# A two-layer SiLU block on one core: zero matmuls at the start, finer loads, plain 128-row matmuls, a split last tile

## The chip, the cores and the metric

The kernel runs on one core of a Trainium2 chip. The metric is the device time of one execution in microseconds (us). Most readings below are taken from a profile of one execution. The span of a profile is about 2 us shorter than the device time of the same execution (135.5 against 137.31 us for the kernel before). Different experiments ran on different chips. Each therefore comes with runs of the kernel before from the same chip, and ratios are taken against those.

## The reference

```python
B, S, D, F = 1, 2048, 640, 1728          # bf16
def reference(x, w1, w2):
    h = jnp.einsum("bsd,df->bsf", x, w1)
    h = silu(h)
    return jnp.einsum("bsf,fd->bsd", h, w2)
```

F is 13.5 times 128. The last block of F has only 64 rows, and both kernels have to deal with that.

## The kernel before

It has two stages, and between them h (transposed, bf16) stays on chip. The w1 stage computes 4 chunks of 512 rows of x times 14 blocks of F. Each block takes five 128x512 matmuls, then a sigmoid on ACT and a product on DVE. The w2 stage computes 16 row tiles of 128 rows. Each row tile has two halves of 320 columns and 13.5 blocks of F.

The start: one x transpose by DMA, then w1 in five row pieces, all from the sync queue.

```python
    nc.sync.dma_start_transpose(out=xT[0][:, :, :], in_=xf[0:NCHUNK, :])     # 512 rows
    for dk in range(DT):                                                     # five pieces of w1
        nc.sync.dma_start(out=w1_sb[:, dk, 0:F], in_=w1r[:, dk, :])
    for c in range(1, SC):
        nc.sync.dma_start_transpose(out=xT[c][:, :, :], in_=...)
    # ... then w2
```

The half block: the last 64 columns of w1 are doubled, so rows 0 to 63 and rows 64 to 127 of the last h block hold the same thing. Output half A takes the lower rows and half B the upper rows, and the two 64-row matmuls can run side by side: both start at 100.58 us in the seam shown below.

```python
        for ft in range(13):
            nc.tensor.matmul(psA[:, :], lhsT=hT_sb[:, ft, s0 : s0 + P], rhs=w2_sb[:, ft, 0:EH], ...)
            nc.tensor.matmul(psB[:, :], lhsT=hT_sb[:, ft, s0 : s0 + P], rhs=w2_sb[:, ft, EH:E], ...)
        nc.tensor.matmul(psA[:, :], lhsT=hT_sb[0:64, 13, s0 : s0 + P],   rhs=w2_sb[0:64, 13, 0:EH], ...)
        nc.tensor.matmul(psB[:, :], lhsT=hT_sb[64:128, 13, s0 : s0 + P], rhs=w2_sb[64:128, 13, EH:E], ...)
        nc.scalar.activation(out=o_sb[:, 0:EH], in_=psA[:, :], func=ACT.Copy)
        nc.vector.tensor_copy(out=o_sb[:, EH:E], in_=psB[:, :])
        nc.sync.dma_start(out=of[s0 : s0 + P, :], in_=o_sb[:, :])
```

## Time and profile before

| | us |
|---|---|
| device time, median of 4 runs | 137.6 (137.3 to 138.24) |
| span of the profile | 135.5 |
| first matmul | 7.32 |
| w2 stage begins | 69.79 |
| last eviction begins | 132.05 |

The page of the kernel before, its busy times and the chain that ended last. TensorE (PE) is the bound, and DVE and ACT are hidden behind it.

```profile
PE 124.3 (92%) x723; PEld 68.5 (51%) x728; DVE 46.2 (34%) x73; ACT 41.5 (31%) x74; POOL 0.7 (0%) x5
PE 92%; DMA 3%; SPq 2%; issue 0%; DVE 0%; DVEq 0%
```

A busy PE is not a PE at full speed. The timeline of the weight loads (PEld) of the kernel before, from the first one on, shows this. Columns: start us, length us, engine, line, operation, operands, count, and in brackets the idle time before with its cause.

```profile
7.31 0.13 PEld L104 LDWEIGHTS <-w_sb 128*128 128x128 bf16 x2 [7.31 <-DMA w_sb<-in_w_dram]
7.72 0.15 PEld L104 LDWEIGHTS <-w_sb 128*128 128x128 bf16 x1 [0.28 <-issue]
8.80 0.13 PEld L104 LDWEIGHTS <-w_sb 128*128 128x128 bf16 x2 [0.93 <-DMA w_sb<-in_w_dram]
...
10.49 0.15 PEld L104 LDWEIGHTS <-w_sb 128*128 128x128 bf16 x1 [0.28 <-issue]
10.92 0.15 PEld L104 LDWEIGHTS <-w_sb 128*128 128x128 bf16 x1 [0.28 <-issue]
11.30 10.68 PEld L104 LDWEIGHTS <-w_sb 128*128 128x128 bf16 x50 [0.23 <-issue]
```

The loads at 10.49 and 10.92 us stand 0.43 us apart with no data wait between them (0.15 us of load and 0.28 of "issue"). From 11.3 us on, 50 follow in 10.68 us, which is 0.216 us from one start to the next. So TensorE ran at half its later pace for the 4.0 us from 7.31 to 11.30; below this is called half clock, or cold. The page's granted-clock row shows full clock in these slices, so on the page the cold stretch can be seen only in the spacing and the durations of the instructions (mostly 634 ns for a matmul, 379 later).

At the warm rate the 280 matmuls of the stage take 60.4 us (280 x 0.2157). The first matmul of the w2 stage, from the timeline of PE:

```profile
69.79 0.30 PE L131 MATMUL psA<-w_sb,hT_sb 128*128 128x320 bf16 x1
```

The second thing to read is the seam between two row tiles, from the timeline of the kernel before:

```profile
100.21 0.30 PE L131 MATMUL psA<-w_sb,hT_sb 128*128 128x320 bf16 x1
100.34 0.30 PE L138 MATMUL psB<-w_sb,hT_sb 128*128 128x320 bf16 x1
100.57 0.09 PEld L148 LDWEIGHTS <-hT_sb 64*128 64x128 bf16 x1 [0.26 <-issue]
100.58 0.31 PE L148 MATMUL psA<-w_sb,hT_sb 64*128 64x320 bf16 x1
100.58 0.31 PE L155 MATMUL psB<-w_sb,hT_sb 64*128 64x320 bf16 x1
100.82 0.31 PE L131 MATMUL psA<-w_sb,hT_sb 128*128 128x320 bf16 x1
100.97 0.30 PE L138 MATMUL psB<-w_sb,hT_sb 128*128 128x320 bf16 x1
```

Read the starts, because the lengths overlap. Plain neighbours start 0.13 to 0.14 us apart. The pair does start at one instant, but 0.24 us after its predecessor, and the next matmul comes another 0.24 us later.

The end of the kernel before, from its timeline: eviction, issue of the store, and then nothing until the span ends at 135.5.

```profile
132.01 0.44 ACT L178 ACTIVATE o_sb<-psA 128x320 bf16<-128x320 f32 x1 [3.44 <-PE psB L155]
132.05 0.49 DVE L179 CAST o_sb<-psB 128x320 bf16<-128x320 f32 x1 [3.39 <-PE psB L155]
132.60 0.33 SPq L180 DMA_DIRECT2D out_dram<-o_sb  x1
```

### The profile page before, as it was taken

Reading aid. Unit: us, or ns where it says so; the run is one execution under the profiler, and the core shown is the slowest. Engines: PE = TensorE matmul, PEld = TensorE weight load, DVE = VectorE, ACT = ScalarE, POOL = GpSimd, SP = SyncE. Lnnn points to the kernel's source line nnn. Section 1 sums busy time; section 2 is a strip of 40 time slices with the busy share of each in tenths; the row PEclk is TensorE's granted clock in tenths of the full one; section 3 lists DMA queues with packets and bytes.
Section 4 is the critical chain, followed back from the end, with each engine's and each line's share of the span. In section 5 each row is a group of like instructions: output and inputs, shape, how many; then the busy total and the mean of one; then the engine's idle time right before and its main releaser. Section 6 shows DMA issues by size and latency. Waiting matters only on the chain.

```text
span 135.5 us, 1791 instructions
## 1 busy us (share of the span) xinstructions
PE 124.3 (92%) x723; PEld 68.5 (51%) x728; DVE 46.2 (34%) x73; ACT 41.5 (31%) x74; POOL 0.7 (0%) x5
## 2 busy tenths in 40 slices
PE   0089999999999999999999999999999999999990
PEld 0024444444444444444456666666666666666650
DVE  0000976666666666666661001111110111111101
ACT  4000855555555555555551001111110011111101
POOL 0001000000000000000000000000000000000000
PEclk9999999999999999999999999999999999999997
DMA  3999999900000000000000111110011111101111
GB/s 69 269 371 316 212 197 303 349 10 0 0 0 2 0 0 5 0 2 0 0 0 0 53 48 48 48 48 23 30 48 48 48 48 53 48 13 36 48 48 48
DMA packets 15239, 9.81 MB, mean 72 GB/s; under 512 B 10752, under 2 KB 14592, under 8 KB 15232
## 3 DMA queue, kind: packets, MB, share of 16 engines
q1 hardware_dynamic: 15232, 9.71, 24.5%
q8 instruction: 5, 0.08, 0.3%
q14 instruction: 2, 0.02, 0.0%
HBM read 4.46 MB, written 2.62 MB: 52 GB/s over the span
## 4 chain that ended last, share of the span: by engine, by line
PE 92%; DMA 3%; SPq 2%; issue 0%; DVE 0%; DVEq 0%
PE ps L104 46%; PE psA L131 22%; PE psB L138 21%; PE psA L148 3%; DMA w_sb<-in_w_dram 3%; SPq L65 2%; DVE o_sb L179 0%; PE psB L155 0%; DVEq L179 0%
## 5 line engine op out<-in xcount | busy, mean ns | idle before, releaser
L104 PE MATMUL ps<-xT,w_sb 128*128 128x512 bf16 x275 | 62.3, 387 | 7.6 <-DMA w_sb<-in_w_dram 7.3
L131 PE MATMUL psA<-w_sb,hT_sb 128*128 128x320 bf16 x208 | 57.1, 300 | 0.0
L138 PE MATMUL psB<-w_sb,hT_sb 128*128 128x320 bf16 x208 | 56.9, 299 | 0.0
L117 DVE TENSOR_TENSOR hT_sb<-ps,sig 128x512 bf16<-128x512 f32 x56 | 38.3, 691 | 32.2 <-ACT sig L112 32.2
L104 PEld LDWEIGHTS <-w_sb 128*128 128x128 bf16 x280 | 27.5, 99 | 41.9 <-DMA w_sb<-in_w_dram 8.8
L112 ACT ACTIVATE sig<-ps 128x512 f32<-128x512 f32 x56 | 33.0, 598 | 35.3 <-PE ps L104 35.3
L179 DVE CAST o_sb<-psB 128x320 bf16<-128x320 f32 x16 | 7.9, 492 | 53.4 <-PE psB L155 53.4
L131 PEld LDWEIGHTS <-hT_sb 128*128 128x128 bf16 x208 | 20.3, 98 | 9.6
L138 PEld LDWEIGHTS <-hT_sb 128*128 128x128 bf16 x208 | 20.4, 98 | 7.4
L178 ACT ACTIVATE o_sb<-psA 128x320 bf16<-128x320 f32 x16 | 7.0, 438 | 54.9 <-PE psB L155 54.9
L148 PE MATMUL psA<-w_sb,hT_sb 64*128 64x320 bf16 x16 | 4.9, 307 | 0.0
L155 PE MATMUL psB<-w_sb,hT_sb 64*128 64x320 bf16 x16 | 4.9, 307 | 0.0
L148 PEld LDWEIGHTS <-hT_sb 64*128 64x128 bf16 x16 | 1.5, 93 | 4.2 <-issue 4.2
L63 ACT ACT_TABLE_LOAD x1 | 1.3, 1283 | 0.7 <-PEq L195 0.7
L155 PEld LDWEIGHTS <-hT_sb 64*128 64x128 bf16 x16 | 1.5, 93 | 0.0
L87 POOL COPY w_sb<-w_sb 128x320 bf16<-128x320 bf16 x1 | 0.5, 451 | 11.8 <-DMA w_sb<-in_w_dram 11.8
L61 DVE MEMSET warm<- 128x1 f32 x1 | 0.1, 59 | 0.8 <-PEq L195 0.8
L63 ACT ACTIVATE warm<-warm 128x1 f32<-128x1 f32 x1 | 0.2, 203 | 0.0
L195 POOL MEMSET const-uint8-127<- 128x1 uint8 x1 | 0.1, 103 | 0.0
L195 POOL MEMSET const-bfloat16-1.0<- 128x1 bf16 x1 | 0.1, 102 | 0.0
L195 POOL MEMSET const-float32-0.0<- 128x1 f32 x1 | 0.1, 99 | 0.2 <-issue 0.2
L195 POOL MEMSET const-float32-1.0<- 128x1 f32 x1 | 0.1, 99 | 0.0
## 6 DMA issues: line engine op xcount, KB each, us to landing
out_dram<-o_sb SPq DMA_DIRECT2D x16, 160.0 KB, 1.8
w_sb<-in_w_dram SPq DMA_DIRECT2D x5, 432.0 KB, 5.2
w_sb<-in_w_dram SPq DMA_DIRECT2D x1, 2080.0 KB, 9.0
w_sb<-in_w_dram SPq DMA_DIRECT2D x1, 80.0 KB, 8.5
xT<-in_x_dram SPq DMA_TRANSPOSE x4, 5.7
w_sb<-in_w_dram SPq DMA_DIRECT2D x1, 40.0 KB, 7.9
```

Of the source, the lines that this page charges most:

```text
L63: nc.scalar.activation(out=warm2[:, :], in_=warm[:, :], func=ACT.Sigmoid)
L65: nc.sync.dma_start_transpose(out=xT[0][:, :, :], in_=xf[0:NCHUNK, :])
L87: nc.gpsimd.tensor_copy(out=w1_sb[:, :, F:F_PAD], in_=w1_sb[:, :, F - F_REM : F],)
L104: nc.tensor.matmul(ps[:fw, :], lhsT=w1_sb[:, dk, f0 : f0 + fw], rhs=xT[c][:, dk, :], start=(dk == 0), stop=(dk == DT - 1),)
L112: nc.scalar.activation(out=sig[:fw, :], in_=ps[:fw, :], func=ACT.Sigmoid,)
L117: nc.vector.tensor_tensor(out=hT_sb[:fw, ft, s0 : s0 + NCHUNK], in0=ps[:fw, :], in1=sig[:fw, :], op=ALU.mult,)
L131: nc.tensor.matmul(psA[:, :], lhsT=hT_sb[:, ft, s0 : s0 + P], rhs=w2_sb[:, ft, 0:EH], start=(ft == 0), stop=(ft == last),)
L138: nc.tensor.matmul(psB[:, :], lhsT=hT_sb[:, ft, s0 : s0 + P], rhs=w2_sb[:, ft, EH:E], start=(ft == 0), stop=(ft == last),)
L148: nc.tensor.matmul(psA[:, :], lhsT=hT_sb[0:F_REM, ft, s0 : s0 + P], rhs=w2_sb[0:F_REM, ft, 0:EH], start=(ft == 0), stop=True,)
L155: nc.tensor.matmul(psB[:, :], lhsT=hT_sb[F_REM : 2 * F_REM, ft, s0 : s0 + P], rhs=w2_sb[F_REM : 2 * F_REM, ft, EH:E], start=(ft == 0), sto ...
L178: nc.scalar.activation(out=o_sb[:, 0:EH], in_=psA[:, :], func=ACT.Copy)
L179: nc.vector.tensor_copy(out=o_sb[:, EH:E], in_=psB[:, :])
```

## The change

It has four parts, with one intent: shorten the parts of PE's chain that are not dense full-speed matmuls.

1. Twelve matmuls on a zeroed tile run while the first loads are under way (warm-up).
2. The first 512 rows of x become two chunks of 256. w1 comes in column blocks of 256, 256, 384 and 832 columns, so that the first block suffices for ten matmuls.
3. The half block of F is padded with zeros to 128 rows. Each row tile but the last (see 4) is then 28 plain matmuls.
4. The last row tile is computed as 320, 160 and 160 columns, each with its own eviction and store, so that only 160 columns remain at the very end.

The core of the diff:

```diff
+    NWARM = 12
+    nc.gpsimd.memset(wz[:, :], 0.0)
+    for i in range(NWARM):
+        nc.tensor.matmul(wps[:, :], lhsT=wz[:, 0:P], rhs=wz[:, :], ...)
+    if F_REM:
+        nc.gpsimd.memset(w1_sb[:, :, F:F_PAD], 0.0)
+        nc.gpsimd.memset(w2_sb[F_REM:P, FT_FULL, :], 0.0)
-    nc.sync.dma_start_transpose(out=xT[0][:, :, :], in_=xf[0:NCHUNK, :])
-    for dk in range(DT):
-        nc.sync.dma_start(out=w1_sb[:, dk, 0:F], in_=w1r[:, dk, :])
-    for c in range(1, SC):
-        nc.sync.dma_start_transpose(...)
+    nc.sync.dma_start_transpose(out=xT[0][:, :, :], in_=xf[s0 : s0 + n0, :])   # 256 rows
+    load_w1(0, 2 * P)
+    load_w1(2 * P, 4 * P)
+    load_w1(4 * P, 7 * P)
+    load_x(1)                                                                 # 256 rows
+    load_w1(7 * P, F)
+    for c in range(2, len(chunks)):
+        load_x(c)                                                             # 512 rows each
...
+    order = [(0, ft) for ft in range(7)] + [(1, ft) for ft in range(7)]
+    order += [(0, ft) for ft in range(7, FT)] + [(1, ft) for ft in range(7, FT)]
+    order += [(c, ft) for c in range(2, len(chunks)) for ft in range(FT)]
...
-            # the pair of 64-row matmuls for the last block of F
+            for ft in range(FT):      # 14 plain blocks, psA and psB
...
+        else:                         # last row tile
+            ranges = [(0, EH), (EH, EQ), (EH + EQ, EQ)]
+            for ri, (e0, ew) in enumerate(ranges):
+                ...                   # 14 matmuls, eviction and store of these columns alone
```

## The prediction

> **What bounds the kernel now.** TensorE: the chain of waits is 92% PE, the rest DMA (3%) and the sync queue (2%) before the first matmul. The timeline shows four stretches of the 135.5 us span:
> - 0 to 7.3 us: PE idle until the first w1 piece lands (wait list).
> - 7.3 to 11.3 us: about 8 matmuls. They last 609 to 634 ns against 379 later: PE is cold, besides two DMA waits (0.93 and 0.54 us).
> - 11.3 to 70 us: w1 stage, one 128x512 matmul per 0.216 us, no gaps. All 280 take 60.4 us: as if started warm at 70.0 - 60.4 = 9.6 us.
> - 70 to 131.9 us: w2 stage, 3.88 us per row tile, then evict, store, finish: 3.6 us.
>
> DVE (34%) and ACT (31%) hide.
>
> **What the change does.**
> 1. Start. The first x transpose has 256 rows, not 512, and w1 comes in column blocks (256, 256, 384, 832), the first enough for ten matmuls. The old transpose held the sync queue 2.77 us; half should hold it 1.5. The first w1 block (327 KB) then lands at about 5.5 us (estimate from 3.7 us issue-to-landing of the old first piece).
> 2. Warm-up. Twelve zero matmuls start once GpSimd has filled their tile, about 1.4 us. [...] Nine cold at 0.427 us and three warm end at 6.0 us; all cold, 6.6. So real work starts at about 6.3 us, warm, with the warm-up, not data, as the last gate.
> 3. Two 256-column chunks: 140 matmuls at about 0.109 us replace 70 at 0.216: +0.2 us. ACT and DVE (estimates 0.38 and 0.43 us, scaled from 598/438 and 691/492 ns) keep under PE's 0.55 us per tile.
> 4. DMA now feeds PE just in time. At 280 GB/s (278 in 2 to 9 us) block 3 lands at 8.2 us against a need at 8.5, x chunk 1 at 9.3 against 10.1. I allow 0.4 us of stalls.
> Stage 1 then ends near 67.2 us: **2.7 us saved**.
> 5. The paired 64-row matmuls go. They are not cheap: from the psB before to the psA after, 0.48 us pass, where plain matmuls at 0.1355 would take 0.407. A tile of 28 plain ones takes 3.79 us instead of 3.88: 0.085 x 15 = **1.3 us saved**.
> 6. Last tile: 28 matmuls of 160 columns. Weight loads last 98 ns, so I take 0.08 us each, not 0.069: +0.3 us, repaid by the shorter last eviction and store. Net 0.
>
> All of it lies on PE's chain.
>
> **Predicted: 133.6 us** (137.6 - 2.7 - 1.3), range 132.3 to 135.2. Faster by over 2%: 0.82; within 2%: 0.17; slower: 0.01.
>
> **What would show it.** First real matmul at 5.8 to 6.7 us, warm durations from the first; waits on w1 or x after it under 0.7 us; stage 2 starting near 67 us; row tiles 3.80 us apart; last tile about 4.1 us; span near 131.5 us.
>
> **What would make it wrong.** The 256-row transpose costs as much as 512, or 512-byte rows crawl: PE stalls after the warm-up, and the gain shrinks to about 2 us. The clock releases later than the warm-up: up to 0.8 us lost. 256-column matmuls bound by weight loads: up to 1 us lost. 160-column ones over 0.1 us: 0.6 lost.

## More of the kernel before

The packed trace also keeps the clock records themselves. The first record of full clock begins at 11.24 us in the kernel before, where the spacing changes; the page counts the time ahead of it as full clock.

## The result

The changed kernel takes 133.55 us (median of 11 runs, 133.35 to 133.94). The kernel before takes 137.63 us (16 runs, 136.81 to 138.55). The ratio is 0.9708, with a 95% interval of 0.9681 to 0.9735. A ratio is the mean time of one kernel's fast runs over that of the other's in the same rounds, so it is not quite the ratio of the medians.

| us | before | changed | saved | predicted |
|---|---|---|---|---|
| first real matmul | 7.32 | 6.78 | | 6.3 |
| w2 stage begins | 69.79 | 67.77 | 2.0 | 2.7 |
| w2 stage begin to last eviction begin | 62.26 | 61.08 | 1.2 | 1.0 |
| last eviction begin to end of span | 3.5 | 2.9 | 0.6 | 0.3 |
| span | 135.5 | 131.7 | 3.8 | 4.0 |

The table compares one execution of each kernel, 137.31 and 133.62 us. The medians lie 4.1 us apart, so about 0.3 us of the gain is missing in this pair. The third and fourth rows regroup what the prediction summed as 1.3 us for fifteen tiles and zero for the last (0.3 lost in it, 0.3 gained behind it).

The page of the changed kernel, the same two lines as before:

```profile
PE 127.0 (96%) x819; PEld 80.2 (61%) x824; DVE 48.7 (37%) x86; ACT 44.6 (34%) x89; POOL 1.8 (1%) x8
PE 91%; DMA 5%; SPq 2%; issue 0%; ACT 0%
```

PE is the bound as before. Its busy time has even grown, because the zero matmuls count. The start, from the timeline of the changed kernel:

```profile
1.31 5.30 PE L75 MATMUL wps<-wz 128*128 128x512 bf16 x12 [1.31 <-POOL wz L72]
5.55 0.15 PEld L75 LDWEIGHTS <-wz 128*128 128x128 bf16 x1 [0.28 <-issue]
6.78 2.19 PEld L128 LDWEIGHTS <-w_sb 128*128 128x128 bf16 x20 [1.07 <-DMA w_sb<-in_w_dram]
6.78 13.42 PE L128 MATMUL ps<-xT,w_sb 128*128 128x256 bf16 x118 [0.17 <-DMA w_sb<-in_w_dram]
9.33 10.70 PEld L128 LDWEIGHTS <-w_sb 128*128 128x128 bf16 x99 [0.36 <-DMA w_sb<-in_w_dram]
67.77 0.30 PE L156 MATMUL psA<-w_sb,hT_sb 128*128 128x320 bf16 x1
```

In this execution all twelve zero matmuls run at half clock (their weight loads start 0.43 us apart). The first record of full clock begins at 7.04 us, 0.26 us after the first real matmul, so the release came barely in time. The loads of the first twenty real ones take 2.19 us, about 0.11 us each, so they are warm but for about the first two. The first waits for its data, and so do the loads at 9.33, by 0.36 us for the third w1 block.

The end, from the timeline of the changed kernel. Only 160 columns are left after the last matmul, and the span ends at 131.7.

```profile
128.85 0.30 ACT L186 ACTIVATE o_sb<-psL 128x160 bf16<-128x160 f32 x1 [1.45 <-PE psL L178]
129.19 0.34 ACTq L189 DMA_DIRECT2D out_dram<-o_sb  x1
```

Issue of the last store to end of span takes 2.5 us instead of 2.9, and the eviction 0.30 us instead of 0.49.

### The profile page after: what moved, and what is told of

The parts are those of the page before. It is cut to its first block, busy times and chain, and to the rows that moved or that the text cites. A ratio compares the mean times of both kernels' runs of the same rounds, so it can differ in the third digit from the quotient of the medians.

```text
span 131.7 us, 2027 instructions
## 1 busy us (share of the span) xinstructions
PE 127.0 (96%) x819; PEld 80.2 (61%) x824; DVE 48.7 (37%) x86; ACT 44.6 (34%) x89; POOL 1.8 (1%) x8
## 4 chain that ended last, share of the span: by engine, by line
PE 91%; DMA 5%; SPq 2%; issue 0%; ACT 0%
PE ps L128 44%; PE psB L163 22%; PE psA L156 22%; DMA w_sb<-in_w_dram 5%; PE psL L178 3%; SPq L93 1%; SPq L96 1%; ACT o_sb L186 0%
## 5 line engine op out<-in xcount | busy, mean ns | idle before, releaser
L128 PE MATMUL ps<-xT,w_sb 128*128 128x512 bf16 (+1 forms) x345 | 60.8, 336 | 0.5 <-DMA w_sb<-in_w_dram 0.2
L141 DVE TENSOR_TENSOR hT_sb<-ps,sig 128x512 bf16<-128x512 f32 (+1 forms) x70 | 41.0, 585 | 28.3 <-ACT sig L136 25.2
L128 PEld LDWEIGHTS <-w_sb 128*128 128x128 bf16 x350 | 34.1, 98 | 27.6 <-DMA w_sb<-in_w_dram 1.4
L136 ACT ACTIVATE sig<-ps 128x512 f32<-128x512 f32 (+1 forms) x70 | 35.8, 512 | 30.1 <-PE ps L128 30.1
L156 PEld LDWEIGHTS <-hT_sb 128*128 128x128 bf16 x210 | 20.5, 98 | 8.1
L163 PEld LDWEIGHTS <-hT_sb 128*128 128x128 bf16 x210 | 20.5, 98 | 8.1
L75 PE MATMUL wps<-wz 128*128 128x512 bf16 x12 | 5.3, 632 | 1.3 <-POOL wz L72 1.3
L75 PEld LDWEIGHTS <-wz 128*128 128x128 bf16 x12 | 1.7, 145 | 4.1 <-issue 2.7
L178 PE MATMUL psL<-w_sb,hT_sb 128*128 128x160 bf16 (+1 forms) x42 | 4.0, 255 | 0.0
L178 PEld LDWEIGHTS <-hT_sb 128*128 128x128 bf16 x42 | 3.4, 98 | 0.6
L186 ACT ACTIVATE o_sb<-psL 128x320 bf16<-128x320 f32 (+1 forms) x2 | 0.7, 371 | 3.0 <-PE psL L178 3.0
L85 POOL MEMSET w_sb<- 64x640 bf16 x1 | 0.6, 630 | 0.1
```

Of the source, the lines that this page charges most:

```text
L75: nc.tensor.matmul(wps[:, :], lhsT=wz[:, 0:P], rhs=wz[:, :], start=(i == 0), stop=(i == NWARM - 1),)
L128: nc.tensor.matmul(ps[:, :n], lhsT=w1_sb[:, dk, f0 : f0 + P], rhs=xT[c][:, dk, :], start=(dk == 0), stop=(dk == DT - 1),)
L136: nc.scalar.activation(out=sig[:, :n], in_=ps[:, :n], func=ACT.Sigmoid,)
L141: nc.vector.tensor_tensor(out=hT_sb[:, ft, s0 : s0 + n], in0=ps[:, :n], in1=sig[:, :n], op=ALU.mult,)
L178: nc.tensor.matmul(pr[:, 0:ew], lhsT=hT_sb[:, ft, s0 : s0 + P], rhs=w2_sb[:, ft, e0 : e0 + ew], start=(ft == 0), stop=(ft == FT - 1),)
```

## The experiments

Two theories stand against each other for the start: the warm-up earns the gain, or the earlier, finer data does. For the w2 stage the question is whether the pair of 64-row matmuls really was dear, and why.

### The parts of the change, one by one

**Plain w2 stage alone**, on the kernel before:

```diff
-    DUP = F_REM == 64
+    DUP = False
+            nc.gpsimd.memset(w1_sb[:, :, F:F_PAD], 0.0)
+            nc.gpsimd.memset(w2_sb[F_REM:P, FT_FULL, :], 0.0)
-        n_full = FT_FULL if F_REM else FT
+        n_full = FT                      # 14 plain blocks, no 64-row matmuls
```

> The kernel before, with the last 64 rows of F padded to 128 by zeros, so that the w2 stage is 28 plain 128-row matmuls per row tile; start and last store untouched. Theory A (the paired 64-row matmuls cost 0.48 us where three plain slots cost 0.407): row tiles 3.80 us apart instead of 3.88, span shorter by 16 x 0.08 = 1.3 us, start unchanged to 0.1 us. Rival B (the pair is free, the shorter row tiles in the changed kernel come from something else there): 28 plain slots plus nothing, tile 3.88 us or longer, span the same.

Measured: 136.19 us against 137.81, ratio 0.9902 (0.9838 to 0.9965). The w2 stage began at 69.79 us, to the digit as before, and its last eviction at 130.90 instead of 132.05. That is 1.15 us less, or 0.07 us per row tile, with the start unchanged. Theory A holds. The prediction's 0.085 us per tile was a little high.

**Warm-up alone**, on the kernel before:

```diff
+    # the twelve zero matmuls of the change, nothing else
```

> The kernel before plus the twelve zero matmuls only. Theory A: first real matmul still at 7.3 us, now at full clock; the w1 pieces that it needs one by one arrive in step, so the w1 stage ends near 7.3 + 60.4 + 0.2 = 67.9 us and the kernel gains about 1.9 us, nearly the whole of the 2.0 us by which the changed kernel starts its w2 stage earlier. Rival B: the last w1 pieces (the fifth was there at 12.1 us) hold the warm TensorE up, and the gain is 0.9 us or less.

Measured: 135.52 us against 137.81, ratio 0.9835 (0.9783 to 0.9888). The start of this kernel, from its timeline of PE:

```profile
1.31 5.30 PE L65 MATMUL wps<-wz 128*128 128x512 bf16 x12 [1.31 <-POOL wz L62]
7.18 1.47 PE L117 MATMUL ps<-xT,w_sb 128*128 128x512 bf16 x6 [0.56 <-DMA w_sb<-in_w_dram]
8.84 7.51 PE L117 MATMUL ps<-xT,w_sb 128*128 128x512 bf16 x33 [0.20 <-DMA w_sb<-in_w_dram]
67.99 0.30 PE L144 MATMUL psA<-w_sb,hT_sb 128*128 128x320 bf16 x1
```

The first six real matmuls, all on the first w1 piece, take 1.47 us including the drain of the last, and the wait for the second piece is only 0.20 us. The w2 stage begins at 67.99 us, against 69.79 before and 67.77 in the changed kernel. Theory A holds: 1.8 of the 2.0 us come with this edit alone. By the ratio the four runs gained 2.3 us, largely because the profiled execution of the kernel before was one of its faster ones.

The edit did more than its text says. The build orders the matmuls itself. In the kernel before, three matmuls use the first w1 piece before PE turns to the second (three weight loads before the wait at 8.80 us); here it is six, one for each of six blocks of F, and that is why the row pieces hardly hold PE up. Was it the clock or the order? In the kernel before the pieces cost PE only 0.23 us (its third and fourth matmul start 0.66 us apart, at 8.15 and 8.81, where 0.43 is the cold distance). A better order at half clock could therefore win about that much; the rest needs the clock. The converse was not run: with three blocks per piece a warm PE would probably have waited longer for data. The next experiment has no such doubt, because with and without its zero matmuls the build puts the real matmuls in the same order.

The four runs lie within 0.13 us (135.46 to 135.59), while the kernel before spread over 1.5 us on the same chip. All four kernels without zero matmuls on that chip spread over 1.5 to 1.75 us, and every kernel with twelve of them over 0.6 us at most. The cold stretch is therefore also what makes the kernel before vary.

**The changed kernel without its warm-up:**

```diff
-    NWARM = 12
-    ... # wz, wps and the twelve matmuls
```

> The changed kernel without its twelve zero matmuls. Theory A (warm-up is what earns the start's gain): first real matmul still at about 6.8 us, but at half clock for about 4 us, 15 of its 256-column matmuls later than with warm-up: w2 stage starts 1.6 to 2.0 us later than 67.8 us, total 1.6 to 2.0 us slower than the changed kernel, its start then within 0.4 us of the kernel before. Rival B (the earlier first data earns it): at most 1 us slower than the changed kernel.

Measured: 135.78 us (134.47 to 136.22), ratio to before 0.9837. It is 2.2 us slower than the changed kernel's 133.55 by the medians, which come from different chips, and 1.8 us by the ratios (0.9837 against 0.9708), which is within what theory A expected. In the profiled execution, the slowest of the four, the w2 stage begins at 70.32 us, later than that of the kernel before. The windows view of this kernel, PE alone (window; us; busy us and count; clock; DMA), shows how long the cold stretch was in the profiled execution:

```profile
11.00:12.00 1.00, 1.00 (x7) 1.00 1.04 399
12.00:13.00 1.00, 1.00 (x8) 1.00 1.27 291
13.00:14.00 1.00, 1.00 (x12) 1.00 1.18 264
```

A window counts a matmul that straddles its edge, so 7 means about five new ones per us, and 12 means about nine. The change of pace comes between 12 and 13 us. The first record of full clock begins at 12.80 us. The first matmul was at 6.78 us, so that is about 6 us of half clock, not 4. The loss of 2.55 us in this execution (70.32 minus 67.77) is larger than expected because the cold stretch was longer, not because the mechanism was another.

How long does the half clock last? In the four traces without zero matmuls, full clock begins 3.5 to 6.0 us after the first matmul. In the seven traces with zero matmuls, a clock record and no idle gap over 0.7 us before the release, it begins 3.0 to 5.7 us after. The record of full clock lasts 122.88 us in the kernel before and 126.29 us in the changed kernel, in both past the last matmul. What sets the moment of the release was not shown. That it varies fits the spread of the cold kernels, and in the changed kernel, where it came 5.7 us after the first zero matmul, twelve of them (5.3 us) were only just enough.

**The changed kernel with the old loads and chunks** (warm-up, plain w2 stage and split last tile kept). It ran next to an unmodified copy of the changed kernel on the same chip:

```diff
-    if S >= 1024:                         # two chunks of 256
+    if False:                             # four chunks of 512
-    load_w1(0, 2 * P)  ... load_x(1) ... load_w1(7 * P, F)
+    for dk in range(DT):
+        nc.sync.dma_start(out=w1_sb[:, dk, 0:F], in_=w1r[:, dk, :])
-    order = [(0, ft) for ft in range(7)] + ...
+    order = [(c, ft) for c in range(len(chunks)) for ft in range(FT)]
```

> The changed kernel itself, as the reference for its two neighbours on the same chip: 133.55 us as before, w2 stage from about 67.7 us.

> The changed kernel with the loads and the chunks of the kernel before (four 512-row transposes, w1 in five row pieces), warm-up, plain w2 stage and split last tile kept. Theory A, from the run with the warm-up alone, whose w2 stage began at 67.99 us against 67.77: the earlier and finer loads are worth 0.2 us, so this kernel is 0.0 to 0.4 us slower than the changed one. Rival B (the loads were planned for something and the single profile hides it): at least 0.8 us slower.

Measured: 133.72 us with the old loads (ratio to before 0.9705) and 133.37 us with the new ones (0.9685). The finer loads, which are most of the diff, are worth 0.28 us by the ratios and 0.35 us by the medians. In the single profiles the w2 stage begins 0.57 us later with the old loads (68.10 against 67.53), still short of rival B's 0.8 us. Theory A holds.

**The changed kernel with an ordinary last tile:**

```diff
-        last_tile = st == ST - 1
+        last_tile = False
```

> The changed kernel with its last row tile treated like the other fifteen (two 320-column halves, one store). The time from the first matmul of the last row tile to the end of the span was 7.45 us before and 6.90 in the changed kernel. Theory A (splitting the last tile so that only 160 columns are left to evict and store at the end earns this): the span grows by about 0.5 us, all of it behind the last row tile's first matmul. Rival B (the end is shorter for another reason, the plain full-height matmuls: 0.08 us): it grows by 0.1 us at most after the last tile's start... that is, the end stays at about 7.0 us.

Measured: 133.97 us (ratio to before 0.9737; the changed kernel had 0.9708 and 0.9685 on two other occasions). Last eviction begin to end of span is 3.4 us (132.0 minus 128.58), as in the kernel before and not the 2.9 of the changed kernel. Theory A holds: the split earns 0.5 us at the end, and up to the last eviction it costs nothing (61.09 us from the begin of the w2 stage with it, 61.11 without).

The parts add up. In per cent of the kernel before: warm-up 1.65, plain w2 stage 0.98, and the last tile 0.3 to 0.5 (the differences from 0.9737). The loads add 0.2. The sum is 3.1 to 3.3, and the whole change measured 2.9 and 3.15. Each ratio is uncertain by 0.3 to 0.7 per cent, so the fit is closer than the data can promise.

### Why the pair was dear

**Both 64-row matmuls on the same rows**, in the kernel before, so that they do not run side by side (in the trace they start 0.14 us apart):

```diff
-                    lhsT=hT_sb[F_REM : 2 * F_REM, ft, s0 : s0 + P],
-                    rhs=w2_sb[F_REM : 2 * F_REM, ft, EH:E],
+                    lhsT=hT_sb[0:F_REM, ft, s0 : s0 + P],
+                    rhs=w2_sb[0:F_REM, ft, EH:E],
```

> The kernel before, but both 64-row matmuls of a row tile read the same lower 64 rows, so they can't run side by side. What makes the pair dear? If the weight loads round it can't be hidden (the trace has 0.26 us before the first of them put down to issue) because two loads for different halves of the array have to follow each other, then two 64-row matmuls in sequence cost two plain slots and the tile is 3.80 us, span shorter by about 1.3 us: pairing loses against doing them one after the other. If a 64-row matmul is dear in itself, the tile is 3.88 us or up to 4.0 and the span the same or up to 2 us longer.

Measured: 140.07 us against 137.81, ratio 1.0151. The theory that pairing itself is what costs is wrong: without it a row tile takes 4.01 us instead of 3.88. The expectation gave such a time to a 64-row matmul that is dear in itself, but the seam of this kernel, from its timeline, says otherwise:

```profile
85.91 0.30 PE L138 MATMUL psB<-w_sb,hT_sb 128*128 128x320 bf16 x1
86.14 0.31 PE L148 MATMUL psA<-w_sb,hT_sb 64*128 64x320 bf16 x1
86.28 0.30 PE L155 MATMUL psB<-w_sb,hT_sb 64*128 64x320 bf16 x1
86.51 0.10 PEld L131 LDWEIGHTS <-hT_sb 128*128 128x128 bf16 x1 [0.26 <-issue]
86.51 0.31 PE L131 MATMUL psA<-w_sb,hT_sb 128*128 128x320 bf16 x1
```

Between the two 64-row matmuls lie 0.14 us, an ordinary slot. Before them and behind them lie 0.23 us each. A 64-row matmul is not dear in itself, but each change between 128-row and 64-row weights is: about 0.10 us over the slot. In the trace the weight load there begins only with its matmul, after 0.26 us of "issue". Between two plain matmuls it begins a whole slot earlier (at 85.77 us in this trace, for the matmul at 85.91). So the pair before did save a slot (0.136 us) but paid for two changes (0.20 us), a net loss of 0.07 us per row tile.

If that is right, the pair pays as soon as two pairs share one change in and one change out.

**Pairs of neighbouring row tiles put next to each other**, on the changed kernel: an even tile ends with its pair and the next odd tile begins with its own. Tiles 14 and 15 stay plain, with zeros beside the duplicated rows of w2.

```diff
+            if st % 2 == 0:
+                steps = full + [(FT_FULL, -1, F_REM)]      # pair last
+            else:
+                steps = [(FT_FULL, -1, F_REM)] + full      # pair first
```

> The changed kernel with the paired 64-row matmuls brought back, but the pairs of two neighbouring row tiles put next to each other (for tiles 0 to 13). Theory A, from the runs so far: a pair does take one slot of 0.136 us instead of two, but each change between 128-row and 64-row weights costs 0.10 us more (0.23 us from start to start); with two pairs between one such change in and one out, two row tiles take 2 x 3.80 - 2 x 0.136 + 2 x 0.10 = 7.53 us instead of 7.60, and the span gets 0.5 us shorter than that of the changed kernel. Rival B (each pair costs its 0.48 us wherever it stands): two row tiles take 7.76 us, the span gets 1.1 us longer.

Measured: 132.80 us (132.70 to 132.83), ratio to before 0.9648. The seam, from the timeline of this kernel:

```profile
70.81 0.30 PE L171 MATMUL psB<-w_sb,hT_sb 128*128 128x320 bf16 x1
71.05 0.31 PE L171 MATMUL psA<-w_sb,hT_sb 64*128 64x320 bf16 x1
71.05 0.31 PE L171 MATMUL psB<-w_sb,hT_sb 64*128 64x320 bf16 x1
71.19 0.30 PE L171 MATMUL psA<-w_sb,hT_sb 64*128 64x320 bf16 x1
71.19 0.30 PE L171 MATMUL psB<-w_sb,hT_sb 64*128 64x320 bf16 x1
71.42 0.31 PE L171 MATMUL psA<-w_sb,hT_sb 128*128 128x320 bf16 x1
```

The two pairs start 0.14 us apart, with one change of 0.24 us in and one of 0.23 us out. The next such seam came 7.54 us later (78.59 us) where 7.53 were expected. The w2 stage up to the last row tile takes 56.6 us (67.42 to 124.05), against 57.05 in the changed kernel. Theory A holds, and this kernel beats both. Of the 0.75 us between the medians, these 0.42 us are the pairs. In the profile the first real matmul also came 0.36 us earlier (6.42 us), as in other executions (6.45 and 6.56 us), so that part is hardly the edit's.

### The start, further

**Eight zero matmuls instead of twelve**, on the changed kernel:

```diff
-    NWARM = 12
+    NWARM = 8
```

> The changed kernel with eight zero matmuls instead of twelve; they end near 4.75 us, 2 us before the first real data. If 3.4 us of activity are enough to release the clock, or the release comes at its usual time whatever TensorE does in the last 2 us, the real matmuls start warm and the time is that of the changed kernel (133.5). If the clock needs activity up to the moment of its release, the real matmuls start cold for some time, and the kernel is 0.5 to 2.5 us slower, with more spread.

Measured: 133.43, 133.56, 133.72 and 134.84 us. Three runs are like the changed kernel; in the fourth, the profiled one, the w2 stage began at 68.83 us, 1.06 late. Neither expectation fits all four runs. In the slow one PE sits idle for 1.74 us before its first real matmul at 6.64 us, and the first record of full clock begins only at 9.90 us, so the real matmuls ran at half clock until then. The three others have no trace; their times say that the clock was up in time. Eight are mostly enough, but not in every execution.

**All of w1 on the scalar queue**, eight zero matmuls:

```diff
-        nc.sync.dma_start(out=w1_sb[:, :, fa:fz], ...)
+        nc.scalar.dma_start(out=w1_sb[:, :, fa:fz], ...)   # all four, before the table load
```

> Eight zero matmuls, and the four w1 loads issued from the scalar queue beside the x transposes on the sync queue. The first w1 block was issued at 2.15 us only because the transpose held the sync queue, and landed at 6.75. Theory A (the queue is what delays it): issued at 0.75 us, it lands near 5 us together with x; real work starts 1.5 us earlier, half of that at half clock, and the 0.36 us wait for the third block goes: about 1.0 us faster than the changed kernel. Rival B (the 16 DMA engines are what delays it, they were busy from 2.3 us on): first real matmul no earlier than 6.3 us, gain under 0.4 us, or a later x.

Measured: 135.79 us, ratio 0.9873, which is 2.2 us slower than the changed kernel. The timeline of PE and PEld of this kernel:

```profile
4.27 0.15 PEld L128 LDWEIGHTS <-w_sb 128*128 128x128 bf16 x1 [0.27 <-DMA w_sb<-in_w_dram]
7.02 5.42 PE L128 MATMUL ps<-xT,w_sb 128*128 128x256 bf16 x35 [2.11 <-DMA xT<-in_x_dram]
13.11 5.09 PE L128 MATMUL ps<-xT,w_sb 128*128 128x256 bf16 x45 [0.67 <-DMA xT<-in_x_dram]
```

And two lines of its windows view, weight loads alone (columns as above):

```profile
9.00:10.00 1.00, 0.67 (x6) 1.00 1.06 366
10.00:11.00 1.00, 0.90 (x10) 1.00 1.10 377
```

The first w1 block is there by 4.3 us, which is what theory A said of the queue. But the x transposes now run beside all of w1: the first lands 6.2 us after issue instead of 3.6, and the second holds PE up again at 13 us. So on the second queue the first w1 block came 2.5 us earlier (4.3 against 6.78 us) and the first transpose 2.6 us later. The late x is less than half of the loss, though. PE sat idle for 2.1 us before its first real matmul at 7.02 us, and until about 10 us the loads come 0.213 us apart instead of 0.109. These 14 or so cold matmuls cost about 1.4 of the 2.1 us by which the w2 stage begins later (69.90 against 67.77). Later data and the second wait account for the rest. So with eight zero matmuls the run does not test the queue alone; with enough of them to fill the gap it was not run.

**Only the first w1 block on the scalar queue**, with the grouped pairs and eight zero matmuls:

```diff
+    load_w1(0, 2 * P, nc.scalar)       # beside the first x transpose
     load_w1(2 * P, 4 * P)              # the rest stays on the sync queue, behind it
```

> The kernel with grouped pairs (132.8 us), with only the first w1 block issued from the scalar queue at 0.75 us, the other blocks behind the first transpose on the sync queue, and eight zero matmuls. In the run with all of w1 on the scalar queue that block landed 3.4 us after issue and the starved transpose was the last to land, at 7.0 us. Theory A (with 327 KB beside it instead of 2.2 MB the transpose of 327 KB is little delayed): both there at about 5.0 us, real work starts 1.4 us earlier, part of it at half clock: 0.6 to 1.2 us faster than 132.8. Rival B (a transpose suffers from any copy beside it, or the half clock takes the gain back): under 0.3 us, or slower.

Measured: 132.26 us (131.98 to 133.40), ratio to before 0.9619, against 133.37 us for the changed kernel on the same chip. Its first real matmul, from the timeline of PE:

```profile
5.57 12.63 PE L135 MATMUL ps<-xT,w_sb 128*128 128x256 bf16 x109 [0.66 <-DMA xT<-in_x_dram]
```

Real work starts 1.2 us earlier than in the changed kernel. The w2 stage begins at 66.75 us, 0.67 earlier than with grouped pairs alone; the ratio moved by 0.3%, the medians by 0.54 us across two chips. That is at the lower edge of what was expected, between the two theories. Full clock begins at 6.49 us here, and 19 real weight loads took 2.49 us where 20 took 2.19 us in the changed kernel, so some of the gain went to the half clock.

**The same with ten zero matmuls:**

> The fastest kernel so far with ten zero matmuls instead of eight, which closes the gap from 4.75 us to the first real matmul at 5.57. One of the four runs with eight took 133.4 us against 132.0 to 132.3, as did one of four of the changed kernel with eight (134.84 against 133.4 to 133.7). If the idle stretch before the first real matmul is what lets the clock stay low in those runs, no run in six lies over 132.9 us; if the release simply comes at a random time after the start, runs near 133 us remain. Median 132.2 in either case.

Measured: 132.32 us (six runs, 132.13 to 132.54), ratio to before 0.9596 (0.9549 to 0.9643). The median is the same and there is no run above 132.54. That fits the idea that the idle gap lets the clock stay low now and then. In the two traces with an idle gap of 1.7 and 2.1 us after eight zero matmuls, the real ones stayed cold until about 10 us, while in all other traces with zero matmuls the clock was up by 7.04 us. But with one outlier in each set of four against none in six, it is not shown. This is the best kernel: 4.0% below the kernel before.

## Why the prediction was right, point by point

The total was predicted at 133.6 us and measured at 133.55. The forecast of where the time lies was right; that the number is met so closely is luck: in the profiles the start was put too high by 0.7 us and the last tile with its end too low by 0.6.

- **What bounds the kernel: right.** Every microsecond taken from PE's chain showed up in the time.
- **Point 1, first block at 5.5 us: wrong by 1.2 us.** The queue was freed on time (the transpose held it 1.36 us; the block was issued at 2.15). But the block took 4.6 us from issue to landing, not the 3.7 of the old first piece. The number also did not follow from its own premise (issue after 0.73 + 1.5 us, then 3.7), which gives 5.9.
- **Point 2, the warm-up: the mechanism was right, the last gate was not.** The zero matmuls ran from 1.31 us at half clock and the real ones were warm but for about the first two. The real start was 6.78 us, not 6.3, and it waited for data, where the prediction had the warm-up as the last gate. The warm-up alone gave 1.8 us in the profile, 2.3 by the runs. The prediction took the release to come at about 4 us, as in the trace of the kernel before (4.0 us); here it came after 5.7, and that the twelve still reached it was a narrow thing.
- **Point 3, 256-column matmuls: right**, at 0.109 us each once warm.
- **Point 4, stalls: right.** The third w1 block held PE up by 0.36 us, against an allowance of 0.4, and no other wait followed.
- **The sum of points 1 to 4 is the mis-sized term:** 2.7 us predicted, 2.0 measured. The prediction could not say which part earned it. The runs do: the warm-up 1.8, the finer loads about 0.2 to 0.35.
- **Point 5, the pair: right in kind,** 0.085 us per tile predicted and 0.07 measured. The prediction gave the cost but not the cause, which is the two changes between weight heights. The pairing itself saves its slot.
- **Point 6, last tile: mis-sized.** The 28 matmuls of 160 columns did not suffer from their weight loads: the last tile took 4.03 us from its first matmul to the last eviction (124.82 to 128.85) against 4.07 before (127.98 to 132.05). The end behind it became 0.6 us shorter, not 0.3. So a net of 0 was predicted for the last tile and its end, and about 0.5 to 0.6 came.

## What to carry to other kernels

Look at the spacing of the first matmuls, not at the busy share: where they stand at twice their later distance (here 0.43 against 0.216 us), put throw-away matmuls under the first loads before rewriting the loads. Here a dozen lines earned 1.8 us and the load rework 0.2 to 0.35. Let the throw-away matmuls run until the data is there: after an idle gap of 1.7 and 2.1 us, two traces show the real matmuls cold until about 10 us. And look at the order that the build made, because a small edit can change it. Packing two half-height matmuls side by side pays only if the slot saved outweighs the two changes of weight height round it (in the kernel before 0.136 us saved against 0.20), so put several such pairs next to each other.

## Hardware figures of these traces

- Full clock began 3.0 to 6.0 us after PE's first matmul in eleven traces: 3.9 in the kernel before, 5.7 in the changed kernel, 6.0 in the changed kernel without warm-up. On one chip the kernel before spread over 1.5 us, with warm-up over 0.13 us.
- In streams of loads and matmuls at full clock, matmuls started 0.216 us apart at 512 columns, 0.109 at 256 and 0.1355 at 320.
- Full-height loads overlap full-height matmuls: in the kernel before the load for the matmul at 130.43 us starts at 130.30, together with the matmul before. At a change between 128-row and 64-row weights the load starts only with its own matmul, and the runs show about 0.10 us per change.
- The first DMA transpose, 256 rows of 640, took 3.6 us from issue to landing with the copies behind it on its own queue (the changed kernel), 4.8 us beside 327 KB of copies from another queue, 6.2 us beside 2.2 MB.
